# A spectral and bilinear-GLU kernel on one core: middle products in pairs, eight inverse products a layer in 12-bit parts, and a new written-out order

## Chip, core and metric

The kernel runs on one core of one Trainium2 chip. The metric is the device time of one execution in microseconds (us). All matrix products run on TensorE (PE); DVE, ACT and POOL (GpSimd) do the elementwise work; SP and ACT issue the DMAs.

## The reference

Two layers, each a spectral filter and a bilinear GLU, with layer norm ahead of both. x is 2048 x 512, the GLU is 1792 wide, all in float32.

```python
def _A_ref(x, w_r, w_i):
    X = rfft2(x, axes=(-2, -1))
    X = X * (w_r + 1j * w_i)
    return irfft2(X, s=(S, D), axes=(-2, -1))

def _B_ref(x, w_gate, w_up, w_down):
    g = einsum("bsd,df->bsf", x, w_gate)
    u = einsum("bsd,df->bsf", x, w_up)
    return einsum("bsf,fd->bsd", g * u, w_down)

x = A_x
x = x + _A_ref(_layernorm(x), A_w_r, A_w_i)
x = x + _B_ref(_layernorm(x), B_w_gate, B_w_up, B_w_down)
x = x + _A_ref(_layernorm(x), A_w_r, A_w_i)
x = x + _B_ref(_layernorm(x), B_w_gate, B_w_up, B_w_down)
```

## The kernel before

x stays in SBUF as `xs`, sixteen tiles of 128 rows by 512. Each layer has these stages.

**Forward.** `fwd` takes one tile: statistics, a twiddle scaled by the norm, four products into `tp`, and copies into the buffer `E`.

**Middle.** `middle(g, ...)` takes one of sixteen groups of `E`. It forms sums and differences `fs` (DVE for groups 0 and 1, POOL for the others), then eight products of 64 columns of weights, in fp32, into the bank `dp`, each into the upper or the lower 64 partitions. ACT copies `dp` to `zs`; one fp32 product across gives `zp`; the filter multiplies it to `ys`; four fp32 products of 128 columns go back into `vq`, which ACT copies into `E`. The filter's complex product has two forms. Form "1" has two half copies on ACT (`jz`), two DVE operations and one POOL product. Form "2" has four DVE operations and no POOL. Two fillers named `wp` stand near the end of the stage, before and after the last `vq`. Each fp32 product shows in the trace as two weight loads and two matmuls.

**Inverse.** `inv(t, ...)` takes one tile of `E`: products into `yi`, then (in the mode "fold") a copy `yb` on ACT and a sum and a difference on DVE into `vs`, then one fp32 product with the tile's twiddle `tw` into `yo`, which DVE adds to `xs` in three pieces; then the statistics for the next norm. Layer by layer, the first eight tiles come right after the middle; the other eight ("second half", `second`) are woven into the GLU's first half.

**GLU.** The operand X is kept as a high and a low part of 12 bits each (type fp32r). `mm3` makes one precise product from three fp32r products: high x high, high x low, low x high. Such parts come from a cast on ACT (high) and a subtraction on POOL or DVE (low). `unit` makes the gate and up products of one 128-wide slice `ft` for one half of the tokens, with a seven-product scheme (banks gx, gy, gw, gz, gv), and in the first half of layer 0 the down product (`db`) from the parts `h`. Its weights are prepared there by `weights` and `down_forms` (POOL, ACT) and stored to memory, and the other three half-layers fetch them; there the down product is a seven-product scheme too (`down`, products ex to ev). Units 0 to 17 of a layer are the first half, from 18 on the second.

**Order.** Every operation is recorded by a planner with what it reads and writes, and the program is issued in an order written out in the file (`ORDER`, packed; `PLACES` gives the buffer of each tile in its ring). Each engine works through its own instructions in that order, so an instruction that waits holds up everything behind it on its engine. `RINGS` gives the number of buffers: "f" are the 128 x 512 temporaries (fs, zs, ys, vs, q, rw and others), "tw" the twiddles, "x", "y", "w", "a", "d" the eight PSUM banks. All instructions are issued by one helper, so the profile puts them on one line, L308; they are told apart by the names of their tiles.

Of the kernel before, what the change touches and what calls it, by code (L numbers as in the profile page):

```python
# [12 lines left out]
F32R = mybir.dt.float32r  # L13
# [15 lines left out]
def consts():  # L29
# [73 lines left out]
SWAPS = "2212212212212212", "2212212212212212"  # L103
FAST = (0, 1)
IDLE = 2, 3
# [7 lines left out]
    'c-k$R2Y6OR*2mA>B#@BM0+Akygc?fdy$AxK7X<{ns4VJQmLeccM5KuFp@;=s7M0@Cq<18A2)%?BAoLC)1xW6k?>Coy^1SbR@7$R)r=S0s8<7Yx{6$KZ8p$IMG#?|6)RVmb`_9n^x=s?z'  # L113
    'dHYCn)oQ4OOGC{x17)D~<Rx?7FCI|1sb!h{K*J<dE^09;Be$XWm=%TPzE+TH`a}z`&s`0dqT=g)cG|9WB_Ds6w22(jqGI))R$|5_jb-(-vR7-e!s=0I<d-l$_n_(MnSf>}_mNVF^;a}P'
    's!53atufL>9<pmjuyY|f2HgnwDkoR;8QICIg8ZfHIjzOc*R+8wW=&zFEi9E}KclBKuT+#x`n;Ue1o(PZuES9SNz<xm=`dre7d4NRmOHv%tBEHi`8?3S^f@Uj|K>ZdT-AEaH^><wH?$zq'
    'JV2I5aNsn0OK)g(Iji&aLuQ7dy@HaWA4_NLBe!%g^gW5wMN$V%8P<mL9VLz6=Onzw$a#&I1MqPG*)lX+%SdsqOG&(J<;hDjkzGg1$GS~hN_B~qeR@ahu)`g6p2VIh8Z8UeQ4g15XzPZ}'
    ';W`${v-Dl`5iSknf?hy|OPa=-4(vEyyP&0KBwLHfG<_XD6XZFrVkBCMuzOWGp)bmMeW=ZtGXg2@u*)PJD_vwW5?7UVT3#mTcvd>yoJ4aGGE4_b34G-g>x@*Ea#$!DPO{N>VfjeE!k5a)'
    'P@ON`p;#AwdNHSxPLQumdud{C;!|lzTSqQyx<2OW1KkKGG15<GK&2VlzpwSBhAv=VCvUd)*Y)fdgC+6@JUWRUp&NJKMrR|>GmLlB9gJSk0lJ)fMa$vRLYGQ{oIxYuc%J)y4A(En73(74'
    'nv~QM=7ue9uGy<nMb@B?+OpQ}m2Ps~mM~lOrY1@OS*9iNqX+m&0lCK05;8?5+Bma?kv)1%>uG+IAlvO_Xq?h2%(`k*;O#Z}k5-miG8=i4khHb*lo4pwT~(EN?Di{Mc9g;<-R{xiTE=vj'
    '6+}UZ?AB@WC-xhyzJ4LARpFp1T5X87o3dv&bg>v+t1iQ@TgzJfuQc(Jt2@xjX&u4!b{!`hb&vLBW=G<uqpX5<DR!PfWVa^vTF3@DXvZM;KJAPKo6CHu4S(&i@;Ir9-d00pqD+??wj~mT'  # L120
    '$~fY!zKmg?1^8oq`IOy$m!I(4dGacrvl;LBlF?V#tpPE4PUGYg`OCg(%IY>5LasOir>gDsudr%4=dndavc*NX?oZ^;)N?Wp9?v6nWpp<PuIK9`O_tx#O+P$4RBAw_7aZ&&10}HbAY;3T'
    'fmzHxP8M3Ejj_){;;0&WuSUi)@+qFQRBOv<G_VJKjWVgZZ=22N!QvzFJWa#Hrx4E%bU35)pgEG2+pw>%N%{#{=TG>46YGwW*7^Y%?+TPYmZ^B=QhDgN)D32>%++<8AHSN4WsAy>`Y*Cf'
    'Lv)f)ZrNfc!(`<~nkcy^(RjF+QRcH;BPC3#EobgauI(VndWQ^Imbfr-N6PCN<awfZiNbW~UR0F|JiE)UkvGU*_t0b!o_OMNXCX;tjm!7xTGWJ@EdL=^KBVVabx&{0bGk(uDVdS`qUO4d'
    'F>PeLx;oMfuegfG*CqE}=h=C3Zf!j*rSvKihhn3WdYPPcRnM|ltcDsR9@o#p$2pDFyhgPubMM*<630ko@>L!5`UiAe1`i<y4r(K!u8cXXMYXiau_vTDlwB0&VBhlS={dM5Nv>EyOf<$D'
    'eIlzXd2Fw~L~ctW>&B7$w&E#Ap_t0E%eos)J8lhjufmwm{RKQGl>D5AAN9g>61i%po5;u2&}Lq#K*nz@TeKC~K-Fc|Xn3xQWIyPeSoVRogWe`>Oa7|@KO4C}i;q5s1yZ#QyQHyqhHlg>'
    '+udx!I+hxAggVoWof_jS%k(ww%gb^VZEOzdtLXTyZDDrn65HGSfaZJ35?j+m;t54egiNrXnOo$uduZ;lmX<V|K?XPIY=LcTYT=b>&_0Hxuh^z$xz<4Q^O2-3+|Ad1l4Mh*Ib%uevB9QO'
    'AKpZ=^Z3Fc^zk1eWgF7o)mN~~Zf!x%kA?ajeMlBuOqOYH*4l6>Yo^&B%xrxdJ#-?IM!-uPmN|{=?Sl%pf!}k~;nL_JKQ*+TG`HUx_SH-{f0jJbktem`JC6Aw=&u4=t-zX8BL5^(%q6p('
    'SEth)D$-6yBhXYOEHIxsSPRc}wY(O)M%g*056@16IQFT#dJG@mW4m(V`(fT$J%*pGpgL8Mzo^tl(NK<WWU1+CLp_5RRFDO%TZ&c(z|~%IXO7<1w`4H*pmi`86y>$G(~LtGwd@76nK_lE'
    'y`5po+bUj~f7O(-Ii@06`zxx;61&SZ!PeE0r#x}G4mwX%{d=aQ7+cQUK&JhYvCe^qw1)Z$^3P4bsdw0~>Fx5bn_jFujQ=LcRKGX5s59ERWR9zgyS1Q~jrf0czQ@Q0zW@^UVBF$S8~lOZ'
    '75}c8f?fJT!^l{!st397hEB5Q%xWD3wp)&0mhm2&OTPMHp}9G8%v-YAAK>lOmHG~uySM!8&-0S>XTPoY6V=0@p_gQiM%$j=Z0wcIK0o>`y={Ig?{7cO8zi6jm%KQ?k+&UfdET?cL3u3O'  # L130
    'O6K{Ey&HH!6%a-`HmWFxn9+t+VO~{q6m9pKa`FcA&)^fEX}Ha%hE4QFlV`ijaNk)d-H(=0-e_s%Q^~!%ekrdc5*>$+H2iFw|AIHqZ{}5$%YGSXs($LX_O|+yJtgxc`+d<*HyP@`>HXnP'
    '@shFeZk=TE<hq$VwXau~XAQhuv_06bDb-nZ)Za(8t15N8pEc6<^^W+{ydi#sml^y<c{%<BZ?wNh8+fl!$A1M$jFk^H#qZ;t(Mi${`Cjr4P-T|+#XL{0`{~$ogg@Q;$Zsv(y;**W4#Nk+'
    '>{#!h&hs03DSicSmH(c%l8CA#V_AO^-%%~+UE}(mcJx|;d-j1-_ak#IzE_bfRzg~$wPYeRl?W^eQcFU%ePnl6H=ma-*k^&p+t<9x)XRhbiSB3ZE<XE__Ofol2b<&T*T~qZ;Hm4-yn*(g'
    ';FUQ<@$dd3Zy6D3q!YgOjj544*Gu%rc`hfMpl&8(<090=6s~VF{|x!#4$=0q940!OqUVM@t;1a?*55^5FDotl5#CKAzdAJ{6smpj+>&I%THxFptWA`aWQ`c;?blxZW2{jIRMUYOPO9th'
    '+66wN@TCw|Tm|24z;AA;>r`%0KOa(|tU5_<YKpW1_1=e`g3pS>TMSo)$jIxZZP1BqA){0!d*!IZZr#WaZ6zhQUdW$N>#cu+)Z@qx@lagGlWoWp&6Df78$%MLre4i09+Ix%e%_GVNO@Hk'
    'gLa<BGu_n_VrU`AH;l+{K=v&p=j1hek=2=KG>;z@5-PK0r0&eU6H*tRucL+K<gVJ%n5vYX8z1tyyh~5<5Kp`W&)<Xa7E2FoaRr*i!DJTX^`^t!AjL(}6p6nEjh#WFHMyNaPSKfIBtMId'
# [88 lines left out]
class Plan:  # L225
# [36 lines left out]
    def order(self):  # L262
# [5 lines left out]
        for i in turn:  # L268
            assert ops[i]["pre"] <= done
            done.add(int(i))  # L270
            for t in ops[i]["tiles"]:
                if not t.placed:
                    t.placed, t.index = True, int(next(places), 16)
# [880 lines left out]
```

## Time and profile before

| | us |
|---|---|
| median of 3 runs | 1072.44 |
| lowest and highest run | 1072.39 and 1073.7 |
| the profiled execution | 1071.4 |
| its span, first to last instruction | 1069.6 |
| PE busy | 1052.7 |
| DVE busy | 814.6 |
| POOL busy | 691.0 |
| ACT busy | 403.7 |

The granted TensorE clock is 1.0 over the span. On the page, the span is cut into 40 slices of 26.7 us. A matmul's duration there overlaps that of the next, so the time that a matmul takes is read from one start to the next.

### The profile page before, as it was taken

Reading aid. Unit: us, or ns where it says so; the run is one execution under the profiler, and the core shown is the slowest. Engines: PE = TensorE matmul, PEld = TensorE weight load, DVE = VectorE, ACT = ScalarE, POOL = GpSimd, SP = SyncE. Lnnn points to the kernel's source line nnn. Section 1 sums busy time; section 2 is a strip of 40 time slices with the busy share of each in tenths; the row PEclk is TensorE's granted clock in tenths of the full one; section 3 lists DMA queues with packets and bytes.
Section 4 is the critical chain, followed back from the end, with each engine's and each line's share of the span. In section 5 each row is a group of like instructions: output and inputs, shape, how many; then the busy total and the mean of one; then the engine's idle time right before and its main releaser. Section 6 shows DMA issues by size and latency. Waiting matters only on the chain.

```text
span 1069.6 us, 18698 instructions
## 1 busy us (share of the span) xinstructions
PE 1052.7 (98%) x6556; PEld 907.5 (85%) x6556; DVE 814.6 (76%) x1603; ACT 403.7 (38%) x965; POOL 691.0 (65%) x888
## 2 busy tenths in 40 slices
PE   8999999999999999999989999999999999999998
PEld 6677888888889888889977779888889998888897
DVE  7677876778876576777897687778888875677688
ACT  6458533334345223223354484222323521222221
POOL 5857788999999454566747136544558983545671
PEclk9999999999999999999999999999999999999999
DMA  9422564779754674657281003555687274563542
GB/s 363 199 70 97 190 235 165 225 263 287 210 182 162 239 231 154 227 168 244 75 317 65 1 18 129 181 196 171 174 296 227 70 238 156 207 241 136 210 143 79
DMA packets 129469, 193.66 MB, mean 181 GB/s; under 512 B 39264, under 2 KB 50784, under 8 KB 127328
## 3 DMA queue, kind: packets, MB, share of 16 engines
q10 hardware_dynamic: 52256, 103.29, 28.3%
q1 hardware_dynamic: 77120, 89.18, 24.8%
q8 instruction: 52, 0.85, 0.3%
q14 instruction: 41, 0.34, 0.1%
HBM read 145.52 MB, written 46.92 MB: 180 GB/s over the span
## 4 chain that ended last, share of the span: by engine, by line
PE 83%; POOL 6%; DVE 6%; DMA 2%; issue 2%; ACT 1%; SPq 0%; DVEq 0%; POOLq 0%; ACTq 0%
PE gz L308 13%; PE gx L308 13%; PE gw L308 6%; PE gy L308 6%; PE gv L308 6%; PE ex L308 5%; PE ez L308 5%; PE db L308 4%; PE dp L308 3%; PE zp L308 3%; PE ew L308 3%; PE yi L308 3%; PE ey L308 3%; PE ev L308 3%; PE tp L308 2%; PE vq L308 2%
## 5 line engine op out<-in xcount | busy, mean ns | idle before, releaser
L308 PE MATMUL gx<-xA,wt 128*128 128x512 f32 (+1 forms) x852 | 180.8, 348 | 0.3 <-DVE xA L308 0.3
L308 PEld LDWEIGHTS gx<-xA,wt 128*128 128x128 f32 x852 | 137.9, 190 | 19.2 <-DVE xA L308 0.5
L308 POOL TENSOR_TENSOR sf<-cc,sf 128x256 fp32r<-128x256 f32 x98 | 72.4, 742 | 65.4 <-ACT sf L308 57.5
L308 POOL TENSOR_TENSOR sf<-q,sf 128x256 fp32r<-128x256 f32 x92 | 67.9, 740 | 65.0 <-ACT sf L308 60.3
L308 DVE TENSOR_TENSOR xs<-xs,db 128x512 f32<-128x512 f32 x128 | 85.5, 682 | 26.7 <-PE db L308 26.4
L308 PE MATMUL db<-wd,h 128*128 128x512 f32 x336 | 92.3, 397 | 0.2 <-POOL h L308 0.2
L308 PE MATMUL gz<-xA,wt 128*128 128x512 f32 (+1 forms) x426 | 90.3, 348 | 0.7 <-DVE c L308 0.7
L308 PE MATMUL gz<-xS,wt 128*128 128x512 f32 (+1 forms) x426 | 90.5, 348 | 0.0
L308 PE MATMUL gy<-xS,wt 128*128 128x512 f32 (+1 forms) x426 | 90.5, 348 | 0.0
L308 PE MATMUL gw<-xS,wt 128*128 128x512 f32 (+1 forms) x426 | 90.2, 347 | 0.0
L308 PE MATMUL gv<-xS,wt 128*128 128x512 f32 (+1 forms) x426 | 89.6, 346 | 0.0
L308 PEld LDWEIGHTS gw<-xS,wt 128*128 128x128 f32 x426 | 69.3, 190 | 10.1 <-issue 0.7
L308 PEld LDWEIGHTS gz<-xS,wt 128*128 128x128 f32 x426 | 69.2, 190 | 10.0 <-issue 0.7
L308 PEld LDWEIGHTS gz<-xA,wt 128*128 128x128 f32 x426 | 68.8, 190 | 10.3 <-DVE c L308 1.1
L308 ACT COPY s<-gx 128x512 f32<-128x512 f32 (+1 forms) x71 | 35.1, 495 | 112.0 <-PE gx L308 106.8
L308 PEld LDWEIGHTS gy<-xS,wt 128*128 128x128 f32 x426 | 68.9, 190 | 9.5 <-issue 0.7
L308 PEld LDWEIGHTS gv<-xS,wt 128*128 128x128 f32 x426 | 68.9, 190 | 8.7
L308 DVE TENSOR_TENSOR q<-gy,s 128x512 f32<-128x512 f32 (+1 forms) x71 | 41.0, 577 | 43.7 <-PE gy L308 31.6
L308 PEld LDWEIGHTS db<-wd,h 128*128 128x128 f32 x336 | 60.9, 189 | 12.9 <-issue 1.5
L308 POOL TENSOR_TENSOR wt<-rg,wt 128x512 fp32r<-128x512 f32 (+1 forms) x56 | 64.0, 1154 | 5.2 <-ACT wt L308 4.5
L308 ACT CAST sf<-q 128x256 fp32r<-128x256 f32 x92 | 37.2, 405 | 74.5 <-DVE q L308 28.9
L308 ACT CAST sf<-cc 128x256 fp32r<-128x256 f32 x98 | 39.2, 406 | 62.8 <-PE ew L308 21.3
(161 smaller groups left out, 2495.3 us busy)
## 6 DMA issues: line engine op xcount, KB each, us to landing
wt<-gu ACTq DMA_DIRECT2D x36, 1024.0 KB, 6.5
wt<-gu ACTq DMA_DIRECT2D x36, 768.0 KB, 5.5
bf<-dn ACTq DMA_DIRECT2D x20, 1024.0 KB, 5.3
wq<-in_wf_dram SPq DMA_DIRECT2D x16, 1024.0 KB, 10.5
bf<-dn ACTq DMA_DIRECT2D x20, 768.0 KB, 4.5
gu<-wt SPq DMA_DIRECT2D x14, 1024.0 KB, 6.7
gu<-wt SPq DMA_DIRECT2D x14, 768.0 KB, 5.8
rg<-in_wb_dram SPq DMA_DIRECT2D x14, 512.0 KB, 4.5
```

The lines of the kernel that those rows point to most:

```text
L308: ins = f(*args, **kw)
```

## The change

The diff, without the packed tables of the order and the places, and without the indentation of lines that only moved:

```diff
-SWAPS = "2212212212212212", "2212212212212212"
+SWAPS = "12" * 8, "12" * 8
+TWOS = [(0,)] + [(g, g + 1) for g in range(1, 15, 2)] + [(15,)]
+SPLIT = True, True
-    RINGS = {"x": 1, "y": 1, "w": 1, "a": 3, "d": 2, "f": 11, "tw": 8, ...
+    RINGS = {"x": 1, "y": 1, "w": 1, "a": 3, "d": 2, "f": 18, "tw": 10, ...
-    def middle(g, E, df, W, due, swap):
...
-        dp = bank("dp", "x")
+    def middles(gs, E, df, W, due, swaps):
+        fss, dps = [], []
+        for g in gs:
...
+            fss.append(fs)
+            dps.append(bank("dp", "x" if g and g == gs[0] else "a"))
         def features():
+            for fs, dp in zip(fss, dps):
                 (the eight products of one group, as before)
-        pe(0.83, features, [(fs, 0), (fs, 1), df, ...], [dp])
+        pe(0.83 * len(gs), features, [*((fs, i) for fs in fss for i in range(2)), df, ...], dps)
+        for g, dp in zip(gs, dps):
+            middle(g, dp, E, W, due(g), swaps[g])
+    def middle(g, dp, E, W, due, swap):
         zs = temp("zs", "f")
...
-        vq = bank("vq", "x" if g == 14 else "w")
+        vq = bank("vq", "wd"[g % 2])
...
-            idle(1, "turn", "d", (256, 512)[g - 14])
+            idle(1, "turn", "a", (256, 512)[g - 14])
-    def inv(t, nm, E, di, mode, tags, due=None, on_act=False, early=None):
+    def inv(t, nm, E, di, mode, tags, due=None, on_act=False, early=None, split=False):
...
-        pe(0.88, lambda: TE.matmul(yo(), tw(), vs(), start=True, stop=True), [tw, (vs, 0), (vs, 1)], [yo])
+        if split:
+            th, tl = (temp("th", "tw", (128, 128), F32R) for _ in range(2))
+            vh, vl = (temp("vh", "f", dt=F32R) for _ in range(2))
+            act(128, lambda: A.copy(th(), tw()), [tw], [th])
+            pool(128, lambda: gtt(tl(), tw(), f32(th()), ALU.subtract), [tw, th], [tl])
+            act(512, lambda: A.copy(vh(), vs()), [(vs, 0), (vs, 1)], [vh])
+            pool(512, lambda: gtt(vl(), vs(), f32(vh()), ALU.subtract), [(vs, 0), (vs, 1), vh], [vl])
+            pe(0.69, lambda: mm3(yo(), th(), tl(), vh(), vl(), True, True), [th, tl, vh, vl], [yo])
+        else:
+            pe(0.88, lambda: TE.matmul(yo(), tw(), vs(), start=True, stop=True), [tw, (vs, 0), (vs, 1)], [yo])
-        for g in range(16):
-            middle(g, E, dcs["f"], W, t0 + BOFF + BSTEP * g, SWAPS[layer][g])
+        for gs in TWOS:
+            middles(gs, E, dcs["f"], W, lambda g: t0 + BOFF + BSTEP * g, SWAPS[layer])
-                inv(t, nms[t], E, dcs["i"], "fold", ("a", "a"), inv2_at(n), early=... )
+                inv(t, nms[t], E, dcs["i"], "fold", ("a", "a"), inv2_at(n), early=..., split=SPLIT[layer])
-    nc = _bacc.Bacc("TRN2", target_bir_lowering=False, num_devices=1)
+    nc = _bacc.Bacc("TRN2", target_bir_lowering=False, num_devices=1, dynamic_dma_scratch_size=1024)
```

Sixteen groups a layer become nine blocks: 0, (1, 2), (3, 4) ... (13, 14), 15. The eight second-half tiles of `inv` in each layer get the split product. `ORDER` and `PLACES` are new throughout. Unpacked, the order of PE's operations in the middle stage of layer 0 is, before and after:

```
before  dp0 dp2 zp0 dp1 zp2 dp5 zp1 dp3 zp5 vq0 dp4 zp3 vq1 dp6 zp4 vq2 dp7 zp6 vq3 dp8 zp7 vq5 dp9 zp8
        vq4 dp11 zp9 vq7 dp10 zp11 vq6 dp12 vq8 zp10 dp14 vq9 zp12 dp13 vq10 zp14 zp13 vq12 dp15 vq11
        zp15 vq13 vq14 wp vq15 wp
after   dp0 dp(1,2) zp0 zp2 dp(5,6) zp1 dp(3,4) zp5 zp3 zp4 dp(7,8) vq2 vq5 zp7 vq0 zp6 vq3 dp(9,10) vq4
        zp8 zp9 vq7 dp(11,12) zp10 zp11 vq8 zp12 dp(13,14) vq9 vq10 zp13 zp14 vq12 dp15 vq1 vq6
        zp15 vq11 vq14 vq13 wp vq15 wp
```

In layer 1 the new order ends with zp15 vq12 vq5 vq13 vq14 wp vq15 wp; the old one with zp15 vq13 vq14 wp vq15 wp.

More of the change, by code (lines that the diff above doesn't have):

```diff
@@ L117 @@
[L117 to L136, printed above, removed]
@@ new lines @@
+    'c-l>x2Xt1&)`s^?LJ5I{-U&q@gkC}?6e)sK0l6Spz}~JPf&~F-f{4PEt0F3jNKtxG1Vk`kXrY6IF5QB(1d@=P+5a;q*R}qv^?lzdb7ppV_ulWG6Okw}Qb;n@e+PO?3vwPMS!$&K-%*mS'
+    '*L7imD%p3nuAJ8!8Y%Z`Y3^OpQgT-d$Ys5UaW&;6PiAXHxvDvuUkb`$tu49XwbNQdipm`=$toALn&g+iG@9q@%Qf{YXJ`p#%Fs$ka83Q3e`$4D!MxepQk)*vI4LK8XeP5+sVq0Nh@@&Q'
+    'DJH)m$u4aq>5RCj<@v26N3<BLokx>OQkbh%(C3o=#TpTu$I4o5!%-8)6-4$5$d#p?<(8&${=0UR3tCxDv;JvTIj7CIb3==n7+tI{B3)UzqDxH;*GdYQBQ954NiBY_>Lo@WVa1BFNQbaq'
+    'W%)vTONJgox;W;HKtpfU&-E!*sUk7hCqnATDJ?3cB%f^2dRXqRUeyHoPzTE(S-_L6S=}IiG*T83#S#z6QB6lGMc!s|7TJqq!SA)dl*JnPu~;Gb8|yYk){?SLt8$i()S0UKjJ%80VzJI~'
@@ L225 @@
 class Plan:
-    RINGS = {"x": 1, "y": 1, "w": 1, "a": 3, "d": 2, "f": 11, "tw": 8, "mv": 8, "rs": 8, "st": 2,
+    RINGS = {"x": 1, "y": 1, "w": 1, "a": 3, "d": 2, "f": 18, "tw": 10, "mv": 8, "rs": 8, "st": 2,
              **{f"{r}{p}": n for p in range(4) for r, n in (("s", SLOTS),)}}
@@ L272, in order @@
                 if not t.placed:
-                    t.placed, t.index = True, int(next(places), 16)
+                    t.placed, t.index = True, int(next(places), 36)
         return [ops[i] for i in turn]
@@ new lines, in middles @@
+    def middles(gs, E, df, W, due, swaps):
+        fss, dps = [], []
+        for g in gs:
+            src = lambda j, g=g: E()[:, :, :, g].rearrange("p (a j) t e -> p a j t e", j=2)[:, :, j]
+            es = [k for t in range(16) for k in ((E, t), (E, t, 0))]
+            fs = temp("fs", "f", (128, 4, 16, 8))
+            for i, op in ((0, ALU.add), (1, ALU.subtract)):
+                args = [*es], [(fs, i), (E, "g", g, i)]
+                if g in FAST:
+                    dve(256, lambda i=i, op=op, fs=fs, src=src: tt(fs()[:, 2 * i:2 * i + 2], src(0), src(1), op), *args, two=True)
+                else:
+                    pool(256, lambda i=i, op=op, fs=fs, src=src: gtt(fs()[:, 2 * i:2 * i + 2], src(0), src(1), op), *args)
+            fss.append(fs)
+            dps.append(bank("dp", "x" if g and g == gs[0] else "a"))
+        def features():
+            for fs, dp in zip(fss, dps):
+                f4 = fs().rearrange("p j t (e q) -> p j (t e) q", q=2)
+                for q in range(2):
+                    for j, c, odd in ((0, 0, 0), (2, 1, 0), (3, 0, 1), (1, 1, 1)):
+                        o = 256 * q + 128 * odd
+                        TE.matmul(dp()[64 * c:64 * c + 64, o:o + 128], f4[:, j, :, q], df()[:, j], start=True, stop=True,
+                                  skip_group_check=True)
+        pe(0.83 * len(gs), features, [*((fs, i) for fs in fss for i in range(2)), df, *(["idle"] if gs[0] == 0 else [])], dps)
+        for g, dp in zip(gs, dps):
+            middle(g, dp, E, W, due(g), swaps[g])
@@ L1028, in second @@
             for n, t in enumerate(o2):
-                inv(t, nms[t], E, dcs["i"], "fold", ("a", "a"), inv2_at(n), early=t1 - 3 if n < EARLY else None)
+                inv(t, nms[t], E, dcs["i"], "fold", ("a", "a"), inv2_at(n), early=t1 - 3 if n < EARLY else None, split=SPLIT[layer])
             st = temp("xf", "e", (128, 4, 8, 2, 128))
```

156 lines of the change are left out of this document (80 added, 76 removed).

## The prediction

> **What bounds the kernel now.** I read the page first: sections 1 and 2, then the chain of work.
>
> ```profile
> span 1069.6 us, 18698 instructions
> ...
> PE 1052.7 (98%) x6556; PEld 907.5 (85%) x6556; DVE 814.6 (76%) x1603; ACT 403.7 (38%) x965; POOL 691.0 (65%) x888
> ...
> POOL 5857788999999454566747136544558983545671
> ...
> PE 83%; POOL 6%; DVE 6%; DMA 2%; issue 2%; ACT 1%; SPq 0%; DVEq 0%; POOLq 0%; ACTq 0%
> ```
>
> TensorE (PE) is busy for 98% of the span, and 83% of the chain is matmuls. So a change gains what it takes from PE's own list, and loses what it makes PE wait. GpSimd (POOL) is second: digits of 9 in the six slices from 187 to 348 us, where layer 0 prepares its weights, and 6% of the chain. Those are the two places to price.
>
> **The change, part by part.**
>
> *1. Two groups' 64-column products together.* The timeline of PE's instructions in the middle stage of layer 0 (start, duration, instruction) and then that of its weight loads:
>
> ```profile
> 38.71 1.10 PE L308 MATMUL dp<-df,fs 128*64 128x128 f32 x16
> ...
> 41.69 1.10 PE L308 MATMUL dp<-df,fs 128*64 128x128 f32 x16
> ...
> 67.52 1.88 PE L308 MATMUL zp<-zs,midt 128*128 128x512 f32 x4
> 69.24 1.13 PE L308 MATMUL vq<-midt,ys 128*128 128x128 f32 x8
> ...
> 72.32 1.02 PE L308 MATMUL zp<-zs,midt 128*128 128x512 f32 x2
> 73.18 2.03 PE L308 MATMUL vq<-midt,ys 128*128 128x128 f32 x16
> 75.05 0.60 PE L308 MATMUL wp<-midt 128*128 128x256 f32 x2
> 76.65 1.13 PE L308 MATMUL vq<-midt,ys 128*128 128x128 f32 x8 [1.00 <-DVE ys L308]
> ```
>
> ```profile
> 38.71 0.86 PEld L308 LDWEIGHTS dp<-df,fs 128*64 128x64 f32 x16
> 39.74 0.30 PEld L308 LDWEIGHTS zp<-zs,midt 128*128 128x128 f32 x2 [0.17 <-issue]
> ```
>
> Durations overlap, so I use start to start. One group (dp, zp, vq) takes 41.69 - 38.71 = 2.98 us. By themselves the three are cheaper: two zp in a row take 69.24 - 67.52 = 1.72, so 0.86 each; two vq in a row take 75.05 - 73.18 = 1.87, so 0.94; the sixteen weight loads of dp take 0.86. That sums to 2.66. So 0.32 us goes with each block of 64-column products: 0.17 of it is the gap before the next full-width load (its row says "issue", it waited for nobody), the rest is the full load that is not hidden behind dp and the dp load not hidden behind its predecessor. The change turns 16 blocks a layer into 9 (seven pairs, groups 0 and 15 alone), so 7 x 2 x 0.32 = 4.5 us leaves PE. No row shows two dp in a row. Bounds: 0 if the second dp of a pair pays as much as a block does now, and 4.5 if it pays nothing. Inside one dp the sixteen loads already alternate between the two column halves without a gap, and a second dp is the same stream going on; so I take 4.5.
>
> [...]
>
> *2. The end of the middle stage.* PE now waits before the last back product, 1.00 us at 76.65 in layer 0, and in layer 1:
>
> ```profile
> 608.86 1.13 PE L308 MATMUL vq<-midt,ys 128*128 128x128 f32 x8 [0.97 <-DVE ys L308]
> ```
>
> Between the start of the last zp and the last vq lie 76.65 - 72.32 = 4.33 us, of which PE works 0.86 + 1.87 + 0.43. The new order, unpacked, puts three vq and the half filler there in layer 0 (0.86 + 2.8 + 0.43 = 4.1) and four vq in layer 1 (5.0). That covers 0.7 and 0.97: 1.7 us, bounds 0 and 1.97. That work is not extra: it is held back from earlier in the stage, where the paired order puts other products.
>
> *3. The product in 12-bit parts*, eight tiles a layer. Now one fp32 product; then three fp32r products as in every other product of the kernel.
>
> ```profile
> 262.31 1.02 PE L308 MATMUL yo<-vs,tw 128*128 128x512 f32 x2
> 262.76 1.95 PE L308 MATMUL db<-wd,h 128*128 128x512 f32 x6
> 264.54 1.54 PE L308 MATMUL gx<-xA,wt 128*128 128x512 f32 x6
> ...
> 274.99 1.52 PE L308 MATMUL db<-wd,h 128*128 128x512 f32 x6
> 276.35 1.52 PE L308 MATMUL gw<-xS,wt 128*128 128x512 f32 x6
> ```
>
> yo and two db (six products) take 264.54 - 262.31 = 2.23; six such products alone take 276.35 - 274.99 = 1.36. So yo costs 0.87 and three products 0.68: 0.19 less in layer 0. In layer 1 the chain of work has six products at 1.39 (start, duration, instruction), so 0.17 there:
>
> ```profile
> 665.34 1.39 PE gw L308 x6
> ```
>
> 8 x 0.19 + 8 x 0.17 = 2.9 us; I take 2.7, since the third weight load has no row in this place. Bounds 2.4 and 2.9.
>
> What it adds lies on ACT and POOL. Rows by shape:
>
> ```profile
> L308 POOL TENSOR_TENSOR wt<-rg,wt 128x512 fp32r<-128x512 f32 x42 | 53.9, 1292 | 1.5 <-ACT wt L308 0.7 <-PE yo L308 0.7
> ...
> L308 POOL TENSOR_TENSOR rg<-rg 128x256 f32<-128x256 f32 x56 | 41.4, 738 | 3.2
> ...
> L308 ACT CAST wt<-rg 128x512 fp32r<-128x512 f32 x42 | 25.9, 620 | 39.4 <-POOL rg L308 36.8 <-PE gz L308 1.7 <-DMA rg<-in_wb_dram 0.9
> ...
> L308 ACT COPY zs<-dp 128x512 f32<-128x512 f32 x32 | 18.7, 585 | 26.3 <-PE dp L308 26.1
> ```
>
> ```profile
> 209.91 2.56 POOL L308 TENSOR_TENSOR wt<-rg,wt 128x512 fp32r<-128x512 f32 x2
> 212.42 1.31 POOL L308 TENSOR_TENSOR h<-q,h 128x512 fp32r<-128x512 f32 x1
> ```
>
> A tile adds one POOL subtraction of 512 (1.26 start to start: two take 212.42 - 209.91 = 2.51) and one of 128 (about 0.44 by the slope from 256 to 512): 1.7 us, and on ACT a cast of 512 (0.62) and one of 128 (about 0.3). yo now waits for the last POOL subtraction, and everything behind yo on PE waits with it; behind yo's result wait the three additions to xs, the statistics, the transpose through memory and POOL's own staging of x.
>
> *4. POOL in layer 0.* In layer 1 this is covered: POOL works 125 of 209 us there. In layer 0 it is not plain. I take the stretch between two marks that both orders have, the first gw of half-unit 3 and that of unit 20:
>
> ```profile
> 128.74 0.87 PE L308 MATMUL gw<-xS,wt 128*128 128x256 f32 x6
> ```
>
> ```profile
> 340.72 0.88 PE L308 MATMUL gw<-xS,wt 128*128 128x256 f32 x6
> ```
>
> ```profile
> 304.81 0.50 PE L308 MATMUL db<-wd,h 128*128 128x512 f32 x1 [0.23 <-POOL h L308]
> ```
>
> ```profile
> 128.70:340.70 212.00, 211.77 (x1080) 179.42 (x1080) 161.93 (x315) 82.71 (x172) 195.16 (x207) 1.00 0.67 221
> ...
> 636.00:845.00 209.00, 208.32 (x1317) 186.78 (x1317) 172.11 (x344) 69.61 (x175) 125.32 (x172) 1.00 0.56 181
> ```
>
> ```profile
> POOL h L308 <- ACT h L308: 6.7, 6, 1.9
> POOL wt L308 <- ACT wt L308: 3.5, 5, 1.4
> POOL u L308 <- ACT u L308: 1.2, 2, 0.7
> POOL xf L308 <- DMA xf<-turns: 1.1, 1, 1.1
> POOL wd L308 <- ACT wd L308: 0.4, 1, 0.4
> ```
>
> POOL is busy 195.2 of 212.0 us, waits 12.9 by its list of waits, and 3.9 are small gaps (212.0 - 195.2 - 12.9). PE waits for POOL once there, 0.23 us for a db. In the new order seven of the eight split tiles fall between the marks: 7 x 1.7 = 11.9 more on POOL, 207.1 in all, while PE's own work falls to about 210.6. The rest of POOL's list between the marks is the same, moved within. So 3.5 us are left for 16.8 us of waits and gaps. The 6.7 us behind ACT's cast of h are waits of a POOL that is ahead of PE, and go when it falls behind. What stays decides: with only the small gaps, 207.1 + 3.9 - 210.6 = 0.4 us of PE waiting; with all but the h waits, 217.2 - 210.6 = 6.6; with everything, 13.3. I take 3.5, the middle of the first two, because the longer ring of temporaries (11 to 18) lets weight raws and casts be held for POOL, but does not remove its waits on ACT and on DMA.
>
> *5. Swap pattern 12 repeated.* Three more groups a layer take form 1 (two half copies on ACT, one POOL product of 512, two DVE operations instead of four). For a pair of groups PE needs 2 x 2.66 + 0.32 = 5.6 us; POOL then 4 x 0.74 + 1.3 = 4.3, ACT 4 x 0.59 + 2 x 0.59 = 3.5, and this row of the stage shows the room on each:
>
> ```profile
> 26.00:78.00 52.00, 50.11 (x425) 35.52 (x424) 38.49 (x60) 26.46 (x48) 36.20 (x52) 1.00 0.38 144
> ```
>
> DVE loses 2 x 0.7 in each swapped group. Zero on the path; a form-1 group that POOL holds up would cost its 1.3.
>
> *6. Longer rings, smaller descriptor scratch, PSUM banks.* No instruction and no DMA is added, and the page's queue section shows no GpSimd queue that would use the scratch. Zero. dp now shares ring a with zp; what that could cost is rival three. The order apart from the above: PE idles 1069.6 - 1052.7 = 17 us in the span; which of these pieces the new order takes or adds can't be read from a row, so I count 0, bounds -1.5 and +1.5 (a tenth of it).
>
> Sum: -4.5 - 1.7 - 2.7 + 3.5 = -5.4. The profiled execution took 1071.4 us (span 1069.6 and 1.8 around it); it lies 1.0 below the median of the runs, 1072.44. From the median: 1067.0.
>
> **The rivals.**
>
> *One: POOL hides everything.* The order fills the waits, and the POOL term is 0: -8.9, 1063.5. For it: before, PE waited on POOL for only 0.23 us although its slices there read 9. Against it: 3.5 us of room for 207 of work.
>
> *Two (the other side): POOL becomes the bound of layer 0's first half.* POOL keeps all its waits and gaps, so the stretch lasts 207.1 + 16.8 = 223.9 instead of 212.0. Layer 0's share of the split gain is swallowed with it; what stays is -4.5 - 1.7 - 1.3 = -7.5, and +11.9 - 7.5 = +4.4: 1076.8. It decides once POOL holds PE up by more than 8.9 us there. For it: the waits on ACT's casts and on DMA are in the trace and don't depend on PE; against it: the h waits do.
>
> *Three: pairing saves nothing.* The second zp of a pair comes while ACT still copies the second dp (zs, 0.59 each), and two dp hold two banks. If each pair waits 0.3 for it, or if the second dp pays 0.32 as a block does, the 4.5 is gone: -1.7 - 2.7 + 3.5 = -0.9, 1071.5. Against it: in the unpacked order a zp or two vq of earlier groups (0.86 to 1.9 us) stand between most pairs and the second zp. [...]
>
> **How the numbers follow.** The forecast 0.50 (own range 1065 to 1070); rival one 0.18; rival two 0.12; rival three 0.15; 0.05 for new waits of the reordered rest, shared between same and slower. A measurement of this kernel can tell about 0.2%, 2.1 us, from no change. Faster, below 1070.3: nearly all of the forecast, rival one, a little of rival three: 0.66. Same: most of rival three and some of the forecast: 0.20. Slower, above 1074.6: rival two and a part of the rest: 0.14. The range 1063 to 1073 leaves out rival two and the tail below rival one.
>
> **What would show it.** Part 1: between the first dp and the last vq of each middle stage, about 2.3 us less; two dp together take 1.7 to 1.9 start to start, not twice the 1.03 from dp to zp. Part 2: the wait before the last vq is gone or under 0.3. Part 3: yo as three products, 0.68. Part 4: POOL's share between the marks at 97% or more, and PE's waits "<-POOL h", "<-POOL wt" or "<-POOL vl" in layer 0 adding up to some 3 us; 0 of them is rival one, over 9 is rival two. The prediction fails if the dp pairs show gaps inside, or if POOL's waits neither shrink nor are covered.

## The result, and the profile after

The changed kernel takes 1065.83 us (median of 4 runs, 1064.08 to 1067.73), the kernel before beside it 1072.41 (4 runs): ratio 0.9937, 95% interval 0.9918 to 0.9956. The prediction was 1067.0, with a range of 1063 to 1073. The profiled execution after took 1066.18, its span 1064.0.

The page of the changed kernel (busy time):

```profile
span 1064.0 us, 18784 instructions
...
PE 1048.2 (99%) x6572; PEld 910.4 (86%) x6572; DVE 806.6 (76%) x1591; ACT 423.1 (40%) x1009; POOL 725.0 (68%) x926
```

PE's busy time fell by 4.5 us, its idle time from 16.9 to 15.8. Where it fell is seen by stage. This is the busy table of before (us, then each engine's busy time) for the middle of layer 0, the middle of layer 1, and the rest of layer 1, each from its first instruction to the next stage's:

```profile
27.55:78.48 50.93, 49.10 (x424) 35.25 (x423) 37.07 (x55) 26.74 (x48) 35.89 (x52) 1.00 0.35 134
559.88:610.68 50.80, 49.06 (x423) 35.70 (x423) 38.23 (x57) 24.49 (x42) 25.76 (x35) 1.00 0.13 47
610.68:1069.60 458.92, 452.61 (x2803) 403.25 (x2802) 354.60 (x669) 144.82 (x363) 256.28 (x344) 1.00 0.51 167
```

and this of after, with the stretch of layer 0 between the two marks of the prediction (gw of half-unit 3, gw of unit 20) first:

```profile
125.60:337.70 212.10, 210.88 (x1075) 179.42 (x1074) 160.07 (x311) 85.96 (x182) 207.70 (x223) 1.00 0.66 216
27.25:75.05 47.80, 46.93 (x424) 35.21 (x423) 33.74 (x50) 29.76 (x53) 37.07 (x50) 1.00 0.40 151
555.30:601.62 46.32, 46.31 (x422) 35.03 (x423) 32.91 (x49) 27.71 (x48) 28.84 (x38) 1.00 0.14 47
601.62:1064.00 462.38, 452.50 (x2811) 404.72 (x2810) 354.50 (x669) 152.65 (x378) 269.32 (x359) 1.00 0.51 166
```

The two middle stages are 3.13 and 4.48 us shorter; PE's busy time in them fell by 2.17 and 2.75, its idle time by 0.96 and 1.73. The stretch between the marks is as long as before (212.0). The rest of layer 1 is 3.46 us *longer*, though its PE work did not grow: its idle time went from 6.3 to 9.9. What is left of the span's 5.6 us lies in layer 0: the stretch from unit 20 to the middle of layer 1 is 1.59 shorter (217.57 against 219.16), the start 0.30 shorter, the stretch from the middle to the first mark 0.26 longer.

The timeline of PE after: the start of a middle stage, a pair of groups, the end of each middle stage, and a product in parts:

```profile
28.12 2.93 PE L313 MATMUL dp<-df,fs 128*64 128x128 f32 x46 [0.43 <-DVE fs L313]
...
32.90 1.97 PE L313 MATMUL dp<-df,fs 128*64 128x128 f32 x32
34.80 1.12 PE L313 MATMUL zp<-zs,midt 128*128 128x512 f32 x2
...
73.25 1.10 PE L313 MATMUL vq<-midt,ys 128*128 128x128 f32 x8
...
178.50 0.84 PE L313 MATMUL yo<-vh,th 128*128 128x512 f32 x3
179.18 1.09 PE L313 MATMUL gw<-xS,wt 128*128 128x512 f32 x4
...
599.80 1.13 PE L313 MATMUL vq<-midt,ys 128*128 128x128 f32 x8
```

A pair takes 34.80 - 32.90 = 1.90 us with no gap inside (the 46 products of the first row are the rest of group 0 and the first pair in one run). Neither last back product (73.25, 599.80) waits any more. The product in parts takes 0.68. And the six largest of PE's waits over the whole span (us in total, times, longest), of which the first, second, fifth and sixth rows were not there before:

```profile
PE gz L313 <- DVE q L313: 1.7, 2, 0.9
PE ex L313 <- ACT u L313: 1.6, 1, 1.6
PE wp L313 <- POOL warm L313: 1.3, 1, 1.3
PE yi L313 <- DVE xs L313: 0.9, 3, 0.4
PE ev L313 <- DVE v L313: 0.8, 1, 0.8
PE ez L313 <- POOL sf L313: 0.8, 1, 0.8
```

Two of them, ex and ez, lie at 796 to 801 us in layer 1. POOL's and then ACT's timeline there tell why:

```profile
795.18 0.74 POOL L313 TENSOR_TENSOR xf<-xf 128x256 f32<-128x256 f32 x1 [5.53 <-DMA xf<-turns]
795.88 0.72 POOL L313 TENSOR_TENSOR sf<-q,sf 128x256 fp32r<-128x256 f32 x1
796.56 2.13 POOL L313 TENSOR_TENSOR xf<-xf 128x256 f32<-128x256 f32 x3
...
799.36 0.72 POOL L313 TENSOR_TENSOR cc<-cc,q 128x256 f32<-128x256 f32 x1
```

```profile
800.11 0.40 ACT L313 CAST sf<-cc 128x256 fp32r<-128x256 f32 x1 [7.29 <-POOL cc L313]
...
800.42 0.58 ACT L313 COPY u<-ex 128x512 f32<-128x512 f32 x1
```

POOL waits 5.53 us for a transfer of staged x; the run with this operation put later shows that nothing that PE needs hangs on it yet. Behind it stand the folded weights sf, for which ez waits, and cc, for which ACT's cast waits 7.29; behind that cast stands ACT's copy of u, for which ex waits 1.56. The wait names ACT; the cause is a transfer two engines further back.

### The profile page after: what moved, and what is told of

It reads as the page before. It is cut to its first block, busy times and chain, and to the rows that moved or that the text cites. A ratio compares the mean times of both kernels' runs of the same rounds, so it can differ in the third digit from the quotient of the medians.

```text
span 1064.0 us, 18784 instructions
## 1 busy us (share of the span) xinstructions
PE 1048.2 (99%) x6572; PEld 910.4 (86%) x6572; DVE 806.6 (76%) x1591; ACT 423.1 (40%) x1009; POOL 725.0 (68%) x926
## 4 chain that ended last, share of the span: by engine, by line
PE 84%; DVE 5%; POOL 4%; DMA 2%; ACT 2%; issue 2%; SPq 1%; DVEq 0%; POOLq 0%; ACTq 0%
PE gx L313 13%; PE gz L313 13%; PE gw L313 7%; PE gv L313 7%; PE gy L313 6%; PE db L313 6%; PE ez L313 5%; PE ex L313 5%; PE yi L313 3%; PE vq L313 3%; PE dp L313 3%; PE ev L313 3%; PE ew L313 3%; PE zp L313 3%; PE ey L313 3%; PE tp L313 2%
## 5 line engine op out<-in xcount | busy, mean ns | idle before, releaser
L313 POOL TENSOR_TENSOR sf<-q,sf 128x256 fp32r<-128x256 f32 x103 | 76.2, 741 | 82.3 <-ACT sf L313 79.1
L313 POOL TENSOR_TENSOR sf<-cc,sf 128x256 fp32r<-128x256 f32 x91 | 67.3, 741 | 52.5 <-ACT sf L313 45.7
L313 ACT CAST sf<-q 128x256 fp32r<-128x256 f32 x103 | 41.5, 406 | 95.9 <-DVE q L313 26.5
L313 DVE TENSOR_TENSOR xs<-xs,yo 128x256 f32<-128x256 f32 (+1 forms) x96 | 45.7, 501 | 21.6 <-PE yo L313 21.3
```

The source lines that it names most:

```text
L313: ins = f(*args, **kw)
```

## The experiments

Nine kernels, each timed beside runs of the kernel before. The packed order differs in each; the diffs show code, or say in words which operations of the order move. Differences from the changed kernel are taken between ratios and are good to about 2.5 us. Spans and stages come from one profiled execution each. Where the order of a stretch is that of the changed kernel, they still differ: the stretch between the marks is 212.16 us in the changed kernel (from the one gw to the other), 211.28 with the pairs taken apart, 212.09 with the last zp later and 211.23 with the staged x later; the rest of layer 1 is 462.38, 462.24 and 461.36 in the first three, and 460.53 in the run with one subtraction twice. So a stage is good to about 1 us between the marks and 2 us in layer 1, except where PE's busy time itself differs.

| run | median us | ratio to before, interval | span |
|---|---|---|---|
| changed kernel | 1065.83 | 0.9937, 0.9918 to 0.9956 | 1064.0 |
| pairs taken apart | 1069.91 | 0.9978, 0.9969 to 0.9987 | 1068.1 |
| full fp32 product, both layers | 1065.35 | 0.9938, 0.9926 to 0.9951 | 1063.4 |
| one subtraction twice, layer 0 | 1074.19 | 1.0018, 1.0009 to 1.0027 | 1071.1 |
| last zp later | 1066.68 | 0.9949, 0.9936 to 0.9963 | 1064.7 |
| before, with the parts alone | 1101.15 | 1.0266, 1.0251 to 1.0282 | 1100.1 |
| staged x later | 1062.59 | 0.9911, 0.9896 to 0.9925 | 1060.3 |
| waits taken out | 1061.18 | 0.9897, 0.9880 to 0.9913 | 1059.4 |
| waits out, parts in layer 1 only | 1061.83 | 0.9902, 0.9887 to 0.9917 | 1061.4 |
| waits out, full fp32 product | 1062.29 | 0.9907, 0.9893 to 0.9921 | 1060.5 |

### Pairs taken apart

```diff
-        pe(0.83 * len(gs), features, [*((fs, i) for fs in fss ...
+        for g, fs, dp in zip(gs, fss, dps):
+            pe(0.83, lambda fs=fs, dp=dp: features(fs, dp), [(fs, 0), (fs, 1), ...
```

> The changed kernel with its pairs taken apart again: the first block of 64-column products stays where the pair stood, the second follows after the next operation of TensorE, all else in the same order. The middle stage then has 13 separate blocks in layer 0 and 15 in layer 1, where the changed kernel has 8 and 8. Theory (each block costs 0.32 us of mode switch and uncovered loads): 12 x 0.32 = 3.8 us slower than the changed kernel, some 1070, with the middle stages 1.6 and 2.2 us longer. Rival (a block costs nothing, the middle stage shrank because the new order fills its waits): within 1 us of the changed kernel, 1066 to 1067, and the middle stages as long as now.

Measured: span 4.1 longer, 4.4 by the ratios (0.0041). The theory holds. The timeline shows blocks standing alone:

```profile
30.62 1.10 PE L307 MATMUL dp<-df,fs 128*64 128x128 f32 x16
31.65 1.13 PE L307 MATMUL zp<-zs,midt 128*128 128x512 f32 x2
32.70 1.10 PE L307 MATMUL dp<-df,fs 128*64 128x128 f32 x16
33.73 1.12 PE L307 MATMUL zp<-zs,midt 128*128 128x512 f32 x2
```

Two dp and two zp take 2 x (32.70 - 30.62) = 4.16 us here; in the changed kernel 1.90 for the pair and 2 x 0.86 for the zp make 3.62. Of the 0.54 between them 0.19 is the way from a zp into a dp (32.70 - 31.65 = 1.05 against 0.86), which the pair pays once as well, ahead of its row; 0.35 is left for the block saved. Twelve more blocks for 4.1 us of span are 0.34 each, the prediction's 0.32. By stages: the middle of layer 0 grew by 1.6 us and that of layer 1 by 3.5, PE's busy time in them by 1.65 and 2.59, together 4.24 or 0.35 a block; the rest are waits, 0.44 of it before the last back product of layer 1. (The span grew by less than the two stages because the stretch between the marks was 0.9 shorter in this execution.)

### The end of the middle stage

The edit is one of order: zp of group 15 behind vq of group 11 in layer 0 and behind vq of group 5 in layer 1.

> The changed kernel with the last zp of each middle stage put later, so that only two back products and the half filler stand between it and the last back product, as in the kernel before (4.33 us there from the last zp to the last vq, 1.0 of it waited). The work moved in front of it is the same, nothing is added. Theory (the three and four back products held for the end cover VectorE's and ACT's work on the last group): the wait before the last back product comes back with 0.7 to 1.0 us a layer, 1.4 to 2.0 us slower in all, 1067.3 to 1067.9. Rival (the wait went because VectorE's swap of the last group became shorter): no wait there above 0.3 us and the time unchanged, 1065.5 to 1066.5.

```profile
74.11 1.13 PE L307 MATMUL vq<-midt,ys 128*128 128x128 f32 x8 [0.71 <-ACT wd L307]
...
601.51 1.13 PE L307 MATMUL vq<-midt,ys 128*128 128x128 f32 x8 [0.83 <-DVE ys L307]
```

Both waits come back, 0.71 and 0.83, and the middle stages are 0.94 and 0.87 longer (48.74 and 47.19). The span shows 0.7 of that and the ratios 1.3 with an uncertainty above it: the place and the size are shown by the stage, the total only by its sign. The wait in layer 0 names ACT's cast of `wd`, a part of the down weights, which the product does not read. That cast ends at 74.11, the last `ys` of DVE at 73.96; which of the two released PE can't be told from the rows, but without the held-back work the wait stands there again.

### The product in parts: what it is worth in this order

```diff
-            th, tl = (temp("th", "tw", (128, 128), F32R) for _ in range(2))
-            vh, vl = (temp("vh", "f", dt=F32R) for _ in range(2))
+            th = temp("th", "tw", (128, 128))
+            vh = temp("vh", "f")
...
-            pool(128, lambda: gtt(tl(), tw(), f32(th()), ALU.subtract), [tw, th], [tl])
...
-            pool(512, lambda: gtt(vl(), vs(), f32(vh()), ALU.subtract), ...
-            pe(0.69, lambda: mm3(yo(), th(), tl(), vh(), vl(), True, True), ...
+            pe(0.88, lambda: TE.matmul(yo(), th(), vh(), start=True, stop=True), ...
```

> The changed kernel with the inverse time product of the second-half tiles as one full fp32 product of ACT's two copies; the two GpSimd subtractions of each tile are gone (16 x 1.7 = 27 us less on GpSimd, half of it in layer 0), the rest of the order stays. Theory (the product in parts is worth 0.17 us a tile on TensorE and GpSimd's added work in layer 0 costs little): 16 x 0.17 = 2.7 slower on TensorE, 0.3 to 1.2 given back where TensorE waited behind GpSimd, so 1067 to 1068.5. Rival (GpSimd's added work is what ate the gain between the two marks of layer 0): no slower than the changed kernel, 1064 to 1066, with layer 0's stretch between the marks 1 us or more shorter and GpSimd near 195 us busy in it.

Between the marks of layer 0, and then from the middle of layer 1 to the end:

```profile
126.00:337.44 211.44, 211.44 (x1067) 178.31 (x1066) 160.26 (x311) 85.99 (x182) 196.32 (x208) 1.00 0.66 217
601.35:1063.40 462.05, 453.84 (x2803) 403.17 (x2802) 354.88 (x669) 152.74 (x378) 257.03 (x344) 1.00 0.51 166
```

No slower than the changed kernel (1065.35 us), and POOL at 196.3 us between the marks: the rival is nearer, though the stretch is 0.66 shorter, not 1 or more. PE has more work (0.56 between the marks, 1.34 in layer 1), but PE's idle time between the marks, 1.22 in the changed kernel, is 0, and in layer 1 it is 8.2 instead of 9.9. So in the order as it was delivered no gain from the parts is seen: 211.44 lies within the 211.23 to 212.16 that the same order with parts takes. The rival's reason is borne out only in small part. Of the 1.22 us between the marks only 0.3 is a wait for POOL; 0.90 is this row of the changed kernel, and behind it these of ACT and of DVE:

```profile
326.96 0.98 PE L313 MATMUL gz<-xS,wt 128*128 128x256 f32 x6 [0.90 <-DVE q L313]
```

```profile
325.04 0.84 ACT L313 CAST xA<-xf 128x768 fp32r<-128x768 f32 x1 [3.21 <-DMA xf<-turns]
...
326.08 0.36 ACT L313 COPY s<-gx 128x256 f32<-128x256 f32 x1
...
326.48 0.42 DVE L313 TENSOR_TENSOR q<-gy,s 128x256 f32<-128x256 f32 x1 [1.87 <-ACT s L313]
```

PE waits for DVE's q, q for ACT's copy of gx, and that copy stands behind a cast that waits 3.21 us for staged x. With the full fp32 product the same cast waits 1.39 and PE does not wait at all. It is a wait of the same kind as that in layer 1. But it is not the parts alone that bring it: in runs with the parts and the same order here, the cast waits 2.55 (last zp later) and 2.40 (staged x later) and PE 0.25 and nothing, and with the pairs taken apart neither waits for the transfer. How late the transfer lands differs from one execution to the next; why, no row shows.

### Is POOL full?

```diff
-            pool(512, lambda: gtt(vl(), vs(), f32(vh()), ALU.subtract), ...
+            for _ in range(1 + (split == "twice")):
+                pool(512, lambda: gtt(vl(), vs(), f32(vh()), ALU.subtract), ...
```

> The changed kernel with GpSimd's 512-column subtraction of the low part done twice in the eight split tiles of layer 0 (the same values again), 8 x 1.26 = 10 us more GpSimd work there, 7 of the 8 between the two marks. Theory (GpSimd, 207.7 of 212.1 us busy between the marks, has 2.0 us of waits and 2.4 of gaps left and is now next to being the bound): of the 8.8 us added between the marks 5 to 9 reach TensorE, 1071 to 1075, with waits behind GpSimd's h, wt or vl. Rival (GpSimd's order has slack that its busy share does not show, because its work is early by many microseconds): under 2 us slower, below 1068.

The theory holds: 8.7 us slower than the changed kernel by the ratios. The stretch between the marks, and PE's and POOL's waits in it:

```profile
125.64:346.67 221.03, 213.77 (x1076) 178.55 (x1074) 160.50 (x311) 85.66 (x182) 216.57 (x229) 1.00 0.63 207
```

```profile
PE db L307 <- POOL h L307: 3.9, 5, 1.4
PE gz L307 <- DVE q L307: 1.7, 2, 1.4
PE yo L307 <- POOL vh L307: 1.6, 2, 1.0
```

```profile
POOL wt L307 <- ACT wt L307: 0.5, 1, 0.5
```

The stretch is 8.9 us longer for 7 x 1.26 = 8.8 us of added work, one for one (6.0 of it is idle time of PE, 2.9 longer busy time at an unchanged clock, which is not explained). POOL is busy 216.6 of 221.0, waits 0.5, and the rest is gaps of some 4 us, which the work does not fill. In the changed kernel it was busy 207.7 of 212.1 with 2.0 of waits: it stood next to the point where added work of POOL goes straight into the time, and had no more than those 2 us left.

### Does the product in parts need the new order?

```diff
-    RINGS = {"x": 1, "y": 1, "w": 1, "a": 3, "d": 2, "f": 11, "tw": 8, ...
+    RINGS = {"x": 1, "y": 1, "w": 1, "a": 3, "d": 2, "f": 15, "tw": 11, ...
-        pe(0.88, lambda: TE.matmul(yo(), tw(), vs(), start=True, stop=True), ...
+        if split:
...
+            pe(0.69, lambda: mm3(yo(), th(), tl(), vh(), vl(), True, True), ...
```

> The kernel before with the product in 12-bit parts alone: the two casts and two subtractions of each second-half tile are put in as soon as the tile's twiddle and both halves of vs are there, everything else keeps the old order; the ring of temporaries grows from 11 to 15, that of twiddles from 8 to 11, the descriptor scratch is cut as in the changed kernel. Theory (in an order that was not made for it, the 1.7 us of POOL and 0.9 us of ACT in front of each product delay it, and in layer 0 POOL fills up): TensorE 2.7 us less, but POOL 7 x 1.7 = 11.9 more between the marks of layer 0 and a chain of 0.6 + 1.3 us in front of some products, 3 to 10 us slower than before. Rival (the old order has the room): 2.7 us faster than before, ratio 0.9975.

Measured: 28.5 us slower than before (0.0266 of 1072.2), far past both expectations. The span grew by 30.5 us; PE's idle time explains 17.2 of it (34.1 against 16.9). Its busy time rose by 13.3, to 1066.0, where 2.7 less was due. Nearly all of the added idle time is three rows of PE's waits:

```profile
PE yo L304 <- ACT vh L304: 6.7, 4, 2.5
PE yo L304 <- POOL vh L304: 5.4, 6, 1.3
PE gx L304 <- ACT s L304: 4.5, 2, 4.2
```

The first two are the theory's own: the product waits for ACT's cast and POOL's subtraction. The third, and the busy time, are seen in windows of 4 us (PEclk is the third number from the end) and in PE's and ACT's timeline:

```profile
116.00:120.00 4.00, 1.99 (x9) 1.99 (x10) 1.82 (x5) 2.97 (x10) 2.44 (x3) 0.58 0.11 26
120.00:124.00 4.00, 4.00 (x20) 3.60 (x20) 1.90 (x6) 1.44 (x5) 1.46 (x3) 0.57 0.00 0
```

```profile
118.01 1.65 PE L304 MATMUL gx<-xA,wt 128*128 128x256 f32 x6 [4.20 <-ACT s L304]
119.46 1.48 PE L304 MATMUL gz<-xS,wt 128*128 128x256 f32 x6
```

```profile
116.87 0.30 ACT L304 CAST th<-tw 128x128 fp32r<-128x128 f32 x1 [3.77 <-DMA tw<-in_ti_dram]
...
117.59 0.36 ACT L304 COPY s<-gx 128x256 f32<-128x256 f32 x1
```

ACT's cast of a twiddle waits 3.77 us for its transfer, a copy that PE needs stands behind it, and PE idles 4.20 us. The granted clock is 0.58 and 0.57 in the two windows from 116 to 124 us. The gate product at 118.01 takes 1.45 us where one takes 0.72 elsewhere, half speed; at that level the two windows make one stretch from 116.6 to 123.4 us (an estimate), and the first product that takes 0.72 again starts at 123.85. So the clock fell some 2.8 us into the wait and came back after some 5.4 us of work. With PE at half speed for that long, the wait of 4.20 us cost some 2.7 us more. Five more such stretches stand in the same trace (from 195, 250, 284, 571 and 676 us), after waits of 1.6 to 3.3 us in sum, broken by products. The granted clock is 0.74 and 0.70 in the two windows of 3 us from 675, which at half speed makes 3.4 us; at 194.67, 250.73 and 283.56 six products have 2.37, 2.67 and 2.49 us where 1.52 is usual, and at 571.22 thirty-two tp take 5.04 us where, in the kernel before, twenty-four take 2.74. At about 3.4 us each, PE works some 22 us at half speed in all six, which makes 11 of the 16 us of unexpected busy time; the other 5 stay open.

The placement was mine: each part as early as its data allow. Another hand-made placement, or longer rings, may cost less; what is shown is only that the parts put into the old order in this way cost 28.5 us.

### The waits taken out

Edit of order in layer 1: the first of POOL's four xf goes behind the next three operations on folded weights (sf, sf and cc in the trace), and the other three behind two more after that.

> The changed kernel with four of POOL's operations on staged x in layer 1 put a few POOL operations later, behind the folded weights sf and cc that they now hold up while one of them waits 5.5 us for its transfer. Theory (that wait is what ACT's cast of sf, ACT's copy of u and TensorE's ez and ex at 796.65 and 801.05 wait for): both waits go, 2.3 us faster than the changed kernel, about 1063.5. Rival (TensorE is only shifted, the time is lost again behind DVE or ACT later in the layer): within 0.7 us of the changed kernel.

Span 3.7 us shorter, 2.8 by the ratios; from the middle of layer 1 to the end 459.58 instead of 462.38 (460.53 in the shortest execution without the moves, so 1 to 2.8 us are the moves'). The theory holds in its rows: no wait of ex or ez is left there, and nothing took its place. POOL still waits for the transfer (3.90), with the folded weights ahead of it.

Then three more swaps of neighbours, the first of them ACT's cast xA of 325.04 behind the copy of gx:

> As the run with the staged x put later, and three more of the new order's waits taken out by a swap of neighbours: in layer 0 ACT's copy of gx (behind which TensorE's gz at 326.96 waits 0.90) goes ahead of the cast xA that waits for a transfer; in layer 1 the ev at 844.37 (0.78) goes behind the next gate product and the gz at 879.76 (0.82) behind the next ez. Theory (these waits are lost time of the new order alone): another 2.3 us, about 1061.3, TensorE's waits under 7 us in all. Rival: the waits come back elsewhere, no more than 0.7 us faster than the run with the staged x alone.

```profile
125.12:335.75 210.63, 210.41 (x1075) 179.70 (x1074) 160.16 (x311) 85.93 (x182) 206.65 (x221) 1.00 0.66 218
600.72:1059.40 458.68, 452.12 (x2811) 404.95 (x2810) 354.76 (x669) 152.80 (x378) 269.35 (x359) 1.00 0.51 167
```

1061.18 us, ratio 0.9897 (0.9880 to 0.9913), 1.5 us below the run before it by the ratios where 2.3 was expected, a difference within the noise; PE's listed waits are 6.6 us in all, as expected under 7. The stretch between the marks is 1.5 us shorter than in the changed kernel, but only 0.6 shorter than in the run with the staged x later, where its order is still the old one; layer 1 lost another 0.9. It has the lowest median of all: 11 us below the kernel before.

### The parts again, with the waits out

The edit is that of the full fp32 product above, made in layer 0 alone and then in both layers, in the order with the waits taken out (layer 0 alone without the swap of ACT's cast xA).

> The same two edits in layer 1 as in the run that takes the waits out, and the product in parts in layer 1 only: layer 0 multiplies ACT's two copies in one full fp32 product, without POOL's two subtractions. Theory (in layer 0 the product in parts gives 1.4 us on TensorE and loses it again behind a GpSimd at 98%): within 0.7 us of the run that takes the waits out, POOL near 196 us between the marks. Rival (with the waits out, the parts are worth their 8 x 0.17 = 1.4 us in layer 0 too): 1.4 us slower than it.

> As the run with the product in parts in layer 1 only, but with the full fp32 product in both layers, in the order with the waits taken out: no part of the split is left, GpSimd's 16 x 1.7 = 27 us are gone. Theory (in the changed kernel TensorE's 16 x 0.17 = 2.7 us were there and were spent in the new order's waits; with the waits out they show): slower than the run that takes the waits out by 2 to 2.7 us, about 1063.5. Rival (the parts give nothing even then, since what they save is lost where the product waits for GpSimd): within 0.8 us of it, 1061 to 1062.

The second of these, with no part of the split left:

```profile
125.27:336.72 211.45, 211.45 (x1068) 178.29 (x1067) 160.20 (x311) 85.81 (x182) 196.06 (x208) 1.00 0.67 217
601.02:1060.50 459.48, 453.33 (x2803) 403.36 (x2802) 354.79 (x669) 152.85 (x378) 256.37 (x344) 1.00 0.51 167
```

Now the parts show: 210.63 against 211.45 between the marks (the run with parts in layer 1 only: 211.44 there) and 458.68 against 459.48 in layer 1 (458.34 with parts in layer 1 only), 0.8 in each; PE's busy time over the whole span is 1.5 us lower with them. The totals order the same way, 1061.18, 1061.83, 1062.29, but differ by less than their intervals. The first run came out within 0.7 us of the waits taken out, as its theory said, but a difference of 0.5 to 0.8 can't be told from its rival's 1.4; in its profile PE is 2.45 us later than with the waits out already at the first dp of layer 0 (29.22 against 26.77), ahead of everything that was edited. For the second neither expectation is met: the parts are worth 1.6 us by the stages, 1.1 by the ratios, not 2.7 and not 0, and the totals alone don't settle it.

## Why the prediction was right

The number was near: 6.6 us faster, where 5.4 was said. Of its terms, the first two hold by runs of their own; that of POOL does not, and part of the agreement is luck.

**Part 1, pairing (-4.5).** Right in mechanism and size. The pair's second dp costs 0.87 and has no gap; taking twelve blocks apart cost 0.34 to 0.35 each, so the fourteen that the change removed are 4.8 to 4.9 us, and PE's busy time in the two middle stages fell by 4.92. What makes up the 0.35 us (the gap of 0.17, the loads that are not hidden, or something else at the switch) was not taken apart. (The order has 8 blocks a layer, from 15: group 0 stands next to the first pair, as it stood next to another group before; the difference is the seven predicted.) Rival three is out.

**Part 2, the end of the middle stage (-1.7).** Right: no wait there now, and 0.94 + 0.87 us of stage when the cover is taken away. The middle stages together gave 7.6 us: 4.9 of busy time, which is part 1, and 2.7 of idle time. The two waits before the last vq were 1.97 of the idle time before. Another 1.60 is a row of PE's waits before that the prediction did not price, and that is gone after; the first of the two is this:

```profile
PE dp L308 <- ACT zs L308: 1.6, 2, 0.8
```

```profile
29.48 1.10 PE L308 MATMUL dp<-df,fs 128*64 128x128 f32 x16 [0.83 <-ACT zs L308]
```

Before, all dp shared the one bank x, so that the second dp of a stage stood waiting for ACT's copy of the first; now they have ring a beside it. Against that stand 0.87 us of new idle time in the middle of layer 0, half of it the 0.43 for DVE's fs at 28.12. Part 6 named the banks and looked for a loss there, in rival three. This is read from the rows, not shown by a run of its own; nor were the swap pattern of part 5 or the longer rings undone by themselves.

**Parts 3 and 4, the product in parts (-2.7 and +3.5, together +0.8).** The net is right, near zero, but each size is too large. PE's busy time does fall by 2.4 us on the page (1050.6 with the full product, 1048.2), and by 1.5 with the waits out, where the stages are 1.6 shorter. POOL is as full as predicted, 207.7 of 212.1 (207.1 of 210.6 was said), and the waits of POOL that count shrank, from 12.9 to 2.0 us: it was "with only the small gaps" that came nearest. PE idles 1.22 us between the marks, not 3.5, and 0.42 to 0.78 in the three other executions of that order. So the step that failed is the term of 3.5, with what was named behind it: 3 us of PE waiting for POOL's h, wt or vl were to be seen, and there is 0.3 for h. The rest came through ACT, whose queue waits for a transfer of staged x. By the prediction's own sign (0 of these waits is rival one) rival one's mechanism came nearest: POOL hid nearly everything. Rival two did not come, but the doubled subtraction shows how close it was, as each further microsecond of POOL's work would have been one of time.

**Part 6, the order (0, bounds -1.5 and +1.5).** Between 0 and 1 us in sum, and this is the part that was seen least. New waits of layer 1 (ex, ez, ev, gz) are 3.9 us by their rows, and the rest of layer 1 is 3.46 longer; earlier waits that went elsewhere (1.6 between unit 20 and the middle of layer 1, some 0.9 net in the middle stages, 0.3 at the start) gave most of that back. The bounds, a tenth of PE's idle time, were too narrow for the pieces and held the sum by luck. That rings and order are free was true of them as delivered, not as a rule: in the old order, at the places it was given there, the product in parts costs 28.5 us.

The sum by stages: -7.6 for the two middles (said: -6.2), +2.0 for everything else (said: +0.8), against -6.6 measured (and -5.6 in span). The +0.8 was to be POOL's 3.5 in layer 0 less 2.7 for the parts; the +2.0 is 3.46 of waits in layer 1, which the prediction had put at nothing, less what went elsewhere. That the one stood in for the other is luck.

## What to carry to other kernels

Price a switch of tile width by start to start times in a row that has it and one that has not; here the 0.32 us a block came out as 0.34 to 0.35 in a run of its own. When a written-out order is replaced, read every wait of the bottleneck engine afterwards and follow each back until it reaches a transfer or an engine that is really late: an operation that waits for a DMA and is not needed yet belongs behind the ones that others wait for; four such moves gave 2.8 us by the ratios, where the whole change gave 6.7. A saving on the bound engine is only visible when nothing else idles it: the same product in parts was worth about 0, 1.1 to 1.6 and minus 28 us in three orders.

## What the runs showed of the hardware

In the kernel before with the parts alone, PE ran at about half speed in six stretches, with a granted clock of 0.58 and 0.57 in the windows of 4 us from 116 us, and of 0.74 and 0.70 in those of 3 us from 675. The first of them lasted for some 5.4 us of work after a wait of 4.20 us, the others for about 3.4 us after waits of 1.6 to 3.3 us in sum; the long one cost some 2.7 us on top of the wait, the others some 1.5 to 1.7 each (estimates from these windows and from the products' times). In the changed kernel, whose longest listed wait of PE is 1.6 us, the granted clock stays at 1.00 in every window of 1 us. But here the length of the waits did not decide it: 0.37, 0.68 and 0.97 us stand ahead of ew, ez and ez at 564.87, 568.25 and 570.17 us with the parts alone, where a slow stretch follows, and the same three ahead of the same products at 542.75, 546.12 and 548.04 in the kernel before, where the clock stays at 1.00. The prediction priced waits at their own length, which came out right in the changed kernel's profile.
